# A gated MLP behind a state-space layer: the first tile of z2 starts among the last sums of v, and its sixteen tiles follow one order

## The chip, the cores and the metric

The kernel runs on one core of a Trainium2 chip. The time is what the device takes for one execution, in microseconds (us); for the kernel before it is 1783.14 us, the median of 3 runs (1782.89 to 1784.71).

Short names of the engines: PE is TensorE (PEld its weight loads), DVE is VectorE, ACT is ScalarE, POOL is GpSimd, SP is SyncE, which only issues transfers.

## The reference

One row of 2048 tokens with 576 channels goes through two layers. Cut to what matters here:

```
x = x + ga * SSM(layernorm(x) * (1 + ca) + sa)      # a convolution over the tokens
h = layernorm(x) * (1 + cb) + sb
z = gelu(h @ w_in)                                  # 2048 x 4608
z1, z2 = z[:, :2304], layernorm(z[:, 2304:])
g = w_sp @ z2 + b_sp[:, None]                       # mixes the 2048 tokens
x = x + gb * ((z1 * g) @ w_out)
```

The change concerns the end of the first layer and the making of z2: for every token, 2304 values of gelu(h @ w_in), and then a layernorm over them.

## The kernel before, in words

**Stages.** The first layer (function `ssm`) is computed by three small Fourier-like steps. Its last step are the sums of v: `y_unit(c, r)` multiplies the stored tensor v with a table on PE (16 small products, or 8 for the narrow fifth chunk `c4`), adds the old x on DVE, and POOL stores the new x1 in DRAM. `c` is one of five chunks of channels, `r` one of four groups of four tiles of 128 tokens. What a `y_unit` needs is loaded by SP: v by `y_vload`, the old x by `y_xload`. For the chunks `c3` and `c4` of the first group the sum goes straight into `x1f`, the buffer `xz` with the first four tiles' rows of x1 (4 x 576 values in each partition).

Next comes `phase_a`. It makes z2 in 16 tiles of 128 tokens, and while it does so prepares other weights on the side. `phase_b` then makes z1 (`z1_unit`), mixes the tokens (`g_products`) and multiplies with w_out.

**One tile b of z2.** The steps and the engines that they run on:

- `ln2_stats(b)`, `roots`, `ln2_rows(b)`: the layernorm of x1, on DVE. The result is the tile `n2` (`n` in the profile).
- `turn(b)`: five transposes on PE into the PSUM tile `pt`. `turn_hi(b)` copies them as float16 (tile `nt`) on ACT, and `turn_lo(b)` puts the rest that float16 leaves out beside it, on DVE.
- `z2_mm(b, h)`, h from 0 to 4: 14 products of 512 columns (256 for h = 4) on PE into a PSUM tile `pz`, of which there are six.
- `z2_gelu(b, h)`: gelu on ACT from `pz` into the SBUF tile `z2` of that token tile (2304 values in each partition, `z` in the profile). The first of them, h = 0, takes a fresh `z2` tile.
- `z2_stats(b, 0..5)`: statistics of z2 on DVE, the last two pieces after `z2_gelu(b, 4)`.
- `roots(b)`: 15 or so tiny operations on DVE that make the two factors of the layernorm. `z2_diff(b)`, for even b alone, subtracts one half of the tile from the other on DVE.
- `z2_norm(b)`: the layernorm itself on ACT, in place. `z2_store(b)`: two transfers of 576 KB that POOL issues, into `z2_d` in DRAM.

Tile b's `roots`, `z2_diff`, `z2_norm` and `z2_store` are written in the pass of the loop for tile b + 1. The pool `zp` of the `z2` tiles has two buffers. So `z2_gelu(b, 0)` cannot begin before the stores of tile b - 2 have landed.

**Side work.** In lists by tile (`side`, `do`), odd tiles take up a block of the left half of w_in: `side_sum` squares it on ACT ahead of `z2_gelu(b, 0)`; `win_scale` sums over partitions with a tiny product on PE ahead of `z2_mm(b, 1)` and makes a scale on DVE; `side_hi` and `side_lo` split the block on ACT and DVE. From tile 3 on ACT also squares pieces of other weights, two for each tile.

**What sets the order.** In the last part of `ssm` and in all of `phase_a` every instruction is pinned: each engine executes in the order in which the program writes it (`Pin`, whose line 132 stands for all of them in the profile). An engine that waits holds up all that is written behind it.

**The weights of z2.** w_in's right half is taken in five blocks of 512 columns: `start_load(q)`, `start_sum(q)` (ACT), `win_scale(5 + q)` (PE, DVE), `start_hi(q)` (ACT), `start_lo(q)` (DVE) make the float16 pair `wz`. Blocks 0 to 2 are done in `ssm`; 3 and 4 are finished beside tile 0 in `phase_a`.

Of the kernel before, what the change touches and what calls it, by code (L numbers as in the profile page):

```python
# [802 lines left out]
class Mlp:  # L803
# [450 lines left out]
    def phase_a(self):  # L1254
        self.prods, self.z1s, self.n2, self.bsp, self.gbs, self.wfs = {}, {}, {}, {}, {}, {}
        ap = self.ap = self.pool(self.c2, "ap", 2)
        cpa = ExitStack()
        self.pa = self.pool(cpa, "pa", 6, space=PSUM)
        self.ps1 = lambda: self.pa.tile([128, 512], F32, name="pz")
        self.zp = self.pool(self.c2, "zp", 2)  # L1260
# [58 lines left out]
        self.z2_mm(0, 0)
        self.start_sum(4)  # L1320
        self.z2_gelu(0, 0)
        self.z2_mm(0, 1)
        self.win_scale(9)
        self.start_hi(4)
        self.z2_gelu(0, 1)
        self.ln2_rows(1)
        self.z2_mm(0, 2)
# [401 lines left out]
```

## Time and profile before

| | before |
|---|---|
| median of 3 runs | 1783.14 us |
| the profiled execution, its time | 1782.85 us |
| the profiled execution, its span | 1781.1 us |
| PE busy | 1693.0 us, 95% of the span |
| DVE busy | 1127.6 us, 63% |
| ACT busy | 784.4 us, 44% |
| transfers, mean | 203 GB/s |

The profile is one execution, and what follows in the text is worked out within it; 1.75 us of its time lie outside the span. A row of the timeline has the start, the duration, the engine, the line (132 for all pinned work), the operation with out<-in, the shape, the count of merged instructions, and in brackets the engine's idle time before it and what ended it. Rows of one group that overlap are merged, so a row's duration over its count is the time from start to start. The durations are us, and those of page section 5 have a mean in ns. A table by windows gives each engine's busy us in a stretch, the granted clock of PE (1.00 is full) and the share of time in which the transfer engines were busy. In the lists of transfers "us to landing" counts from the end of the issue.

The stretch of interest lies between 415 us, where the last sums of v begin, and 698 us, where `g_products` begins. PE starts on z2 at 439.46 us and on z1 at 679.70 us.

### The profile page before, as it was taken

Reading aid. Unit: us, or ns where it says so; the run is one execution under the profiler, and the core shown is the slowest. Engines: PE = TensorE matmul, PEld = TensorE weight load, DVE = VectorE, ACT = ScalarE, POOL = GpSimd, SP = SyncE. Lnnn points to the kernel's source line nnn. Section 1 sums busy time; section 2 is a strip of 40 time slices with the busy share of each in tenths; the row PEclk is TensorE's granted clock in tenths of the full one; section 3 lists DMA queues with packets and bytes.
Section 4 is the critical chain, followed back from the end, with each engine's and each line's share of the span. In section 5 each row is a group of like instructions: output and inputs, shape, how many; then the busy total and the mean of one; then the engine's idle time right before and its main releaser. Section 6 shows DMA issues by size and latency. Waiting matters only on the chain.

```text
span 1781.1 us, 34047 instructions
## 1 busy us (share of the span) xinstructions
PE 1693.0 (95%) x14202; PEld 1195.6 (67%) x14202; DVE 1127.6 (63%) x2242; ACT 784.4 (44%) x1023; POOL 223.7 (13%) x350
## 2 busy tenths in 40 slices
PE   5688999997999999999999999999999999999999
PEld 1344555565455456877787777887778787787787
DVE  7988999868888997998783544483222274222322
ACT  5668999854576665554341322241211132011110
POOL 1221232342122110000000000000000000000000
PEclk8788999998999999999999999999999999999999
DMA  8457545799588888786554666563655572545520
GB/s 277 139 207 235 145 129 161 192 248 301 163 278 264 277 235 259 284 283 245 207 206 166 238 234 222 202 255 101 216 203 187 176 271 70 182 174 175 201 84 27
DMA packets 145866, 361.57 MB, mean 203 GB/s; under 512 B 23296, under 2 KB 59008, under 8 KB 143792
## 3 DMA queue, kind: packets, MB, share of 16 engines
q1 hardware_dynamic: 103104, 167.30, 29.8%
q0 software_dynamic: 33120, 153.95, 25.8%
q10 hardware_dynamic: 9488, 38.16, 5.4%
q8 instruction: 111, 1.82, 0.4%
q14 instruction: 43, 0.35, 0.1%
HBM read 256.86 MB, written 93.05 MB: 196 GB/s over the span
## 4 chain that ended last, share of the span: by engine, by line
PE 53%; issue 10%; DVE 9%; DMA 7%; ACT 2%; POOL 1%; SPq 0%; POOLq 0%; ACTq 0%; DVEq 0%
PE ps L1451 9%; PE ps L1453 9%; PE ps L1452 9%; PE ps L1416 9%; PE pz L132 4%; PE ps L1505 3%; PE ps L1506 3%; PE ps L1503 3%; DMA zset<-set_d 2%; DVE zset L1134 2%; DMA z_d<-z 1%; DVE bsz L132 1%; DVE gt L1466 1%; ACT z L132 1%; DMA gbs<-in_w_out 1%
## 5 line engine op out<-in xcount | busy, mean ns | idle before, releaser
L1451 PE MATMUL ps<-wsp,zset 128*128 128x256 f16 x2016 | 550.2, 273 | 2.9 <-DVE gt L1466 2.8
L1453 PE MATMUL ps<-wsp,zset 128*128 128x256 f16 x2016 | 550.1, 273 | 1.4 <-DVE zset L1134 1.3
L1452 PE MATMUL ps<-wsp,zset 128*128 128x256 f16 x2016 | 550.1, 273 | 0.0
L132 PE MATMUL pz<-wz,nt 128*128 128x512 f16 (+1 forms) x1120 | 224.2, 360 | 8.1 <-ACT nt L132 6.7
L1466 DVE SCALAR_TENSOR_TENSOR gt<-ps,sc,bsp 128x512 f32<-128x512 f32 x33 | 24.7, 749 | 317.2 <-PE ps L1453 317.2
L1416 PE MATMUL ps<-n2q,wf 128*128 128x512 f16 x1008 | 223.1, 379 | 0.0
L1451 PEld LDWEIGHTS <-zset 128*128 128x128 f16 x2016 | 197.7, 98 | 29.8 <-DVE gt L1466 3.0
L1452 PEld LDWEIGHTS <-zset 128*128 128x128 f16 x2016 | 197.5, 98 | 26.2
L1453 PEld LDWEIGHTS <-zset 128*128 128x128 f16 x2016 | 197.5, 98 | 25.0 <-DVE zset L1134 2.0
L132 PEld LDWEIGHTS <-nt 128*128 128x128 f16 x1120 | 109.5, 99 | 114.1 <-ACT nt L132 8.4
L1416 PEld LDWEIGHTS <-wf 128*128 128x128 f16 x1008 | 98.6, 98 | 111.8
L1428 POOL DMA_DIRECT2D zset<-set_d x96 | 50.8, 529 | 969.3 <-PE ps L1453 742.5
L1421 ACT ACTIVATE z<-ps,sc 128x512 f32<-128x512 f32 x56 | 37.8, 681 | 280.5 <-PE ps L1416 278.0
L1505 PE MATMUL ps<-wout,z 128*128 128x288 f16 x448 | 127.6, 286 | 0.0
L1506 PE MATMUL ps<-wout,z 128*128 128x288 f16 x448 | 127.6, 286 | 0.0
L1503 PE MATMUL ps<-wout,z 128*128 128x288 f16 x448 | 126.0, 286 | 1.0 <-ACT ot L1513 1.0
L1466 DVE SCALAR_TENSOR_TENSOR gt<-ps,sc,gt 128x512 f32<-128x512 f32 (+1 forms) x165 | 111.8, 694 | 5.4
L1134 DVE TENSOR_TENSOR zset<-raw,zset 128x1024 f16<-128x1024 f32 x48 | 58.5, 1220 | 75.2 <-ACT zset L1133 75.2
L1133 ACT ACTIVATE zset<-raw 128x1024 f16<-128x1024 f32 x48 | 50.3, 1050 | 99.6 <-PE ps L1453 69.7
L132 ACT ACTIVATE z<-pz,sc 128x512 f32<-128x512 f32 (+1 forms) x80 | 49.4, 647 | 54.1 <-DMA z_d<-z 43.6
L1521 DVE TENSOR_TENSOR ot<-ot,ps 128x288 f32<-128x288 f32 x31 | 14.0, 452 | 78.7 <-ACT ot L1513 78.7
L369 PE MATMUL ps<-ln_x,r1t 128*128 128x288 f32 x128 | 42.7, 490 | 18.9 <-issue 12.4
(360 smaller groups left out, 2830.6 us busy)
## 6 DMA issues: line engine op xcount, KB each, us to landing
zset<-set_d POOLq DMA_DIRECT2D x96, 896.0 KB, 4.8
set_d<-zset ACTq DMA_DIRECT2D x36, 896.0 KB, 5.8
raw<-z_d SPq DMA_DIRECT2D x48, 512.0 KB, 4.6
wf<-win_d SPq DMA_DIRECT2D x72, 320.0 KB, 3.5
raw<-in_w_spT SPq DMA_DIRECT2D x43, 512.0 KB, 6.3
z_d<-z POOLq DMA_DIRECT2D x32, 576.0 KB, 7.6
u_d<-st1o POOLq DMA_DIRECT2D x16, 576.0 KB, 4.5
u<-u_d SPq DMA_DIRECT2D x36, 256.0 KB, 4.7
```

The lines of the kernel that those rows point to most:

```text
L132: return self.tc.keep_in_program_order(f(*a, **k))
L1133: nc.scalar.activation(o[:, k, 0], t, AF.Copy)
L1134: nc.vector.tensor_tensor(o[:, k, 1], t, o[:, k, 0], op=ALU.subtract)
L1416: nc.tensor.matmul(pm.rearrange("p (t c) -> p t c", t=4), w[:, kw], self.n2[q][:, :, kn], start=i == 0, stop=i == len(Z1) - 1)
L1428: self.nc.gpsimd.dma_start(o, self.set_d[n // 4, n % 4])
L1451: T.matmul(pm, z[:, a, 0, c], w[:, b, 0], start=i + half == 0, stop=False, skip_group_check=True)
L1452: T.matmul(pm, z[:, a, 0, c], w[:, b, 1], start=False, stop=False, skip_group_check=True)
L1453: T.matmul(pm, z[:, a, 1, c], w[:, b, 0], start=False, stop=i == 7, skip_group_check=True)
L1466: V.scalar_tensor_tensor(dst, pm, inv, to, op0=ALU.mult, op1=ALU.add)
L1503: T.matmul(pl, p[:, 1, ts], w[:, 0, hs], start=st, stop=sp)
L1505: T.matmul(pa, p[:, 0, ts], w[:, 0, hs], start=st, stop=False)
L1506: T.matmul(pa, p[:, 0, ts], w[:, 1, hs], start=False, stop=sp)
```

## The change: what it does

1. `z2_mm(0, 0)` to `z2_mm(0, 2)` of the first tile move from `phase_a` into `ssm`. They stand among the last seven `y_unit`s: after `z2_mm(0, 0)` come three of them, after `z2_mm(0, 1)` two, after `z2_mm(0, 2)` two. `y_unit(c4, 0)`, the last part of the first tiles' rows, is taken ahead of `win_scale(8)`; `start_lo(2)` moves behind the first products. SP loads v for `c4` earlier and the old x of four `y_unit`s later.
2. PSUM changes hands at that place: the pool `psp` of `ssm` is closed, and the pool `pa` of `phase_a` opened, before `win_scale(8)`. The pools `zp` and `np` are opened earlier too, where the pool `wpre` is closed.
3. All tiles from 1 to 15 follow the order that only tile 1 had: `z2_mm(b, 1)`, `turn(b + 1)`, `z2_gelu(b, 1)`, `turn_hi(b + 1)` and `turn_lo(b + 1)` are written ahead of `roots(b - 1)`, `z2_diff`, `z2_norm(b - 1)` and `z2_store(b - 1)`.
4. The z2 tiles 2 and 5 use the buffer `x1f` instead of one of the two of `zp`. So tiles 3 to 7 wait for the stores of the tile three before them. From tile 8 on `x1f` holds blocks of w_sp, and the rotation is by two as before.
5. The three `nt` buffers are now two of `ap` and one of `np`.

The core of the diff:

```
+        first.close()
+        mlp.open_z2()
...
         y_unit(c2, 2)
         mlp.start_sum(3)
-        mlp.start_lo(2)
+        y_unit(c4, 0)
...
+        mlp.pair_stats(1)
+        mlp.ln2_rows(0)
+        banks.close()
+        ps1 = mlp.open_banks()
         mlp.win_scale(8)
+        mlp.turn(0)
+        mlp.turn_hi(0)
         mlp.start_hi(3)
+        mlp.turn_lo(0)
+        mlp.z2_mm(0, 0)
+        mlp.start_lo(2)
+        mlp.z2_gelu(0, 0)
+        for c, r in ((c2, 3), (c3, 1), (c4, 1)):
+            y_unit(c, r)
...
+        mlp.start_sum(4)
+        mlp.z2_mm(0, 1)
+        mlp.z2_gelu(0, 1)
+        mlp.start_lo(3)
+        y_unit(c3, 2)
+        y_unit(c4, 2)
+        mlp.win_scale(9)
+        mlp.start_hi(4)
+        mlp.z2_mm(0, 2)
+        mlp.z2_gelu(0, 2)
+        mlp.ln2_rows(1)
+        y_unit(c3, 3)
+        y_unit(c4, 3)
...
         if h == 0:
-            self.zs[b] = self.zp.tile([128, FH], F32, name="z2")
+            self.zs[b] = self.x1f.rearrange("p b d -> p (b d)") if b in (2, 5) else self.zp.tile([128, FH], F32, name="z2")
...
             self.z2_stats(b - 1, 5)
-            if b == 1:
-                do(b, PE)
-                self.z2_mm(b, 1)
+            do(b, PE)
+            self.z2_mm(b, 1)
+            if b + 1 < 16:
                 self.turn(b + 1)
-                self.z2_gelu(b, 1)
+            self.z2_gelu(b, 1)
+            if b + 1 < 16:
                 self.turn_hi(b + 1)
                 self.turn_lo(b + 1)
             self.roots(b - 1, b + 2 if b + 2 < 16 else None)
...
-            if b > 1:
-                do(b, PE)
-                self.z2_mm(b, 1)
-                if b + 1 < 16:
-                    self.turn(b + 1)
-                self.z2_gelu(b, 1)
             self.z2_store(b - 1)
             do(b, V0)
             self.z2_stats(b, 0, 1)
-            if 2 < b + 1 < 16:
-                self.turn_hi(b + 1)
-                self.turn_lo(b + 1)
             self.z2_mm(b, 2)
```

How instructions stand now, at three places. First PE at the start of z2. Before, the last of all sums (`ue` is v of chunk c4, `u` that of c3) stands right ahead of the transposes of tile 0 (`pt`):

```order
L132 MATMUL pk<-u_4585,st_1879 64x128
L132 MATMUL pk<-ue,st_1879 64x64 x8
L132 MATMUL pt<-ident,n_4616 128x128 x5
L132 LDWEIGHTS nt
L132 MATMUL pz<-wz,nt 128x512
```

Now it is the sum of c4 for the first group, and the tiny product of `win_scale(8)` follows it:

```order
L132 MATMUL pk<-u_4470,st_1879 64x128
L132 MATMUL pk<-u_4471,st_1879 64x128
L132 MATMUL pk<-ue,st_1879 64x64 x8
L132 MATMUL pz<-acc,ones 128x1
L132 MATMUL pt<-ident,n_4599 128x128 x5
L132 LDWEIGHTS n_4626
L132 MATMUL pz<-wz,n_4626 128x512
```

Seven sums that stood ahead of the transposes stand behind them.

Second ACT in tile 8. Before: two squares of side weights, `z2_gelu(8, 0)`, then `z2_norm(7)` (in place on the 2304 values of tile 7), `z2_gelu(8, 1)`, the two copies of `turn_hi(9)`, and the other gelus:

```order
L132 ACTIVATE wsst,acc<-wsst 128x864 x2
L132 ACTIVATE z_6053<-pz,sc 128x512
L132 ACTIVATE z_5867<-z_5867,nm_6075,r_6074 128x2304
L132 ACTIVATE z_6053<-pz,sc 128x512
L132 ACTIVATE nt<-pt 128x512
L132 ACTIVATE nt<-pt 128x128
L132 ACTIVATE z_6053<-pz,sc 128x512 x2
```

Now:

```order
L132 ACTIVATE wsst,acc<-wsst 128x864 x2
L132 ACTIVATE z_6054<-pz,sc 128x512 x2
L132 ACTIVATE n_6080<-pt 128x512
L132 ACTIVATE n_6080<-pt 128x128
L132 ACTIVATE z_5868<-z_5868,nm_6104,r_6103 128x2304
L132 ACTIVATE z_6054<-pz,sc 128x512 x2
```

The norm of tile 7 went from behind the first gelu to behind the second and behind `turn_hi(9)`.

Third DVE in tile 9. Before, the last statistics of tile 8 (`bsz`) are followed at once by `roots(8)` (`BN_AGGR` and what follows):

```order
L132 BN_STATS bsz<-z_6053 128x6 x2
L132 BN_AGGR mvx<-bsz 128x2
L132 TENSOR_SCALAR vh_6208<-mvx 128x2
L132 TENSOR_SCALAR rq_6209<-vh_6208 128x2
L132 TENSOR_SCALAR rx<-rq_6209 128x2
```

Now the end of the scale of `win_scale` and the two operations of `turn_lo(10)` (`nt<-pt`) stand right ahead of it:

```order
L132 TENSOR_TENSOR sc<-sc 128x1
L132 TENSOR_TENSOR nt<-pt,nt 128x512
L132 TENSOR_TENSOR nt<-pt,nt 64x128
L132 BN_AGGR mvx<-bsz 128x2
L132 TENSOR_SCALAR vh_6250<-mvx 128x2
```

`roots(b - 1)` moved behind `turn_lo(b + 1)` on DVE.

More of the change, by code (lines that the diff above doesn't have):

```diff
@@ L153, in ssm @@
         kp = ctx.enter_context(tc.tile_pool(name="kp", reuse_waits="tile", bufs=2, side="right"))
-        psp = ctx.enter_context(tc.tile_pool(name="psp", bufs=2, space=PSUM, reuse_waits="tile"))
+        banks = ctx.enter_context(ExitStack())
+        psp = banks.enter_context(tc.tile_pool(name="psp", bufs=2, space=PSUM, reuse_waits="tile"))
         early = ctx.enter_context(ExitStack())
@@ L619, in ssm @@
                 sb = ctx.enter_context(tc.tile_pool(name="sb", reuse_waits="tile", bufs=2, side="right"))
-                wpre = ctx.enter_context(tc.tile_pool(name="wpre", reuse_waits="tile", bufs=2, side="right"))
+                first = ctx.enter_context(ExitStack())
+                wpre = first.enter_context(tc.tile_pool(name="wpre", reuse_waits="tile", bufs=2, side="right"))
             if 9 <= tick < 13:
@@ L730, in ssm @@
         v_unit(c4, 3)
+        first.close()
+        mlp.open_z2()
         mlp.sum_two(2)
         y_vload(c2, 2)
-        for c, r in ((c2, 2), (c2, 3), (c3, 1), (c3, 2), (c3, 3), (c4, 1), (c4, 2), (c4, 3)):
+        y_xload(c2, 2)
+        y_vload(c4, 0)
+        for r in range(1, 4):
+            y_xload(c4, r)
+        for c, r in ((c2, 3), (c3, 1)):
             y_xload(c, r)
-        y_vload(c4, 0)
-        y_vload(c2, 3)
-        y_vload(c3, 1)
+            y_vload(c, r)
         y_vload(c4, 1)
+        mlp.start_load(4)
+        y_xload(c3, 2)
+        y_xload(c3, 3)
         mlp.start_rows()
         y_unit(c3, 0)
+        mlp.pair_stats(0)
         mlp.win_scale(7)
@@ L901, in start, with open_z2, open_banks @@
         self.stg = self.pool(self.c2, "stg", 2)
+    def open_z2(self):
+        self.zp = self.pool(self.c2, "zp", 2)
+        self.np = self.pool(self.c2, "np", 1)
+        self.ap = self.wzp
+    def open_banks(self):
+        self.cpa = ExitStack()
+        self.pa = self.pool(self.cpa, "pa", 6, space=PSUM)
+        self.ps1 = lambda: self.pa.tile([128, 512], F32, name="pz")
+        return self.ps1
     def start_x1(self):
@@ L1205, in turn_hi @@
         A, pm = self.nc.scalar, self.tps[b]
-        nt = self.nts[b] = self.ap.tile([128, 9, 128], F16, name="nt", bufs=3)
+        nt = self.nts[b] = self.ap.tile([128, 9, 128], F16, name="nt") if b % 3 else self.np.tile([128, 9, 128], F16, name="n0")
         A.activation(nt[:, 0:4], pm[:, 0].rearrange("p (k c) -> p k c", k=4), AF.Copy)
@@ L1256, in phase_a @@
         ap = self.ap = self.pool(self.c2, "ap", 2)
[L1257 to L1260, printed above, removed]
         self.wp = self.pool(self.ctx, "wp", 7, side="right")
@@ L1311, in phase_a @@
             side(12, LD, self.z1_load, 0, f)
-        self.turn(0)
-        self.turn_hi(0)
         self.x1_load(4)
-        self.turn_lo(0)
-        self.start_lo(3)
         do(0, LD)
[L1319 to L1327, printed above, removed]
         self.start_lo(4)
-        self.z2_gelu(0, 2)
         self.z2_mm(0, 3)
@@ L1387, in phase_a @@
             self.z2_gelu(b, 4)
-        cpa.close()
+        self.cpa.close()
         self.z2_stats(15, 5)
```

10 lines of the change are left out of this document (removed).

## The prediction, made before the changed kernel was run

> **What bounds the kernel now.** I read the page first: PE is busy for 95% of the span, so time is lost only where PE waits. Its groups name two such waits for z2 (line 132), and ACT's gelus wait mostly for the stores of z2.
>
> ```profile
> PE 1693.0 (95%) x14202; PEld 1195.6 (67%) x14202; DVE 1127.6 (63%) x2242; ACT 784.4 (44%) x1023; POOL 223.7 (13%) x350
> L132 PE MATMUL pz<-wz,nt 128*128 128x512 f16 (+1 forms) x1120 | 224.2, 360 | 8.1 <-ACT nt L132 6.7
> L132 ACT ACTIVATE z<-pz,sc 128x512 f32<-128x512 f32 (+1 forms) x80 | 49.4, 647 | 54.1 <-DMA z_d<-z 43.6
> ```
>
> Then the windows, for where PE is idle: 8.5 us of 20 ahead of z2, and almost nothing late in z2.
>
> ```profile
> 420.00:440.00 20.00, 11.46 (x139) 9.01 (x135) 15.69 (x48) 6.32 (x4) 5.56 (x8) 0.74 1.03 285
> 612.00:680.00 68.00, 65.53 (x349) 34.11 (x348) 61.37 (x185) 44.48 (x62) 12.37 (x14) 1.00 0.85 247
> ```
>
> Last PE's timeline. One tile without waits takes 14.2 us (462.08 to 476.24). The one large wait is 4.21 us, and the 14 products behind it take 4.88 us instead of 3.18.
>
> ```profile
> 440.91 6.22 PE L132 MATMUL pz<-wz,nt 128*128 128x512 f16 x28 [0.69 <-ACT nt L132]
> 447.11 6.20 PE L132 MATMUL pz<-wz,nt 128*128 128x512 f16 x28
> 453.15 0.71 PE L132 MATMUL pt<-ident,n 128*128 128x128 f32 x5
> 462.08 13.78 PE L132 MATMUL pz<-wz,nt 128*128 128x512 f16 x70
> 476.24 7.73 PE L132 MATMUL pz<-wz,nt 128*128 128x512 f16 x42
> 488.18 4.88 PE L132 MATMUL pz<-wz,nt 128*128 128x512 f16 x14 [4.21 <-ACT nt L132]
> 492.90 0.28 PE L132 MATMUL pz<-acc,ones 128*128 128x1 f32 x2
> 493.04 3.18 PE L132 MATMUL pz<-wz,nt 128*128 128x512 f16 x14
> ```
>
> A second loop runs beside PE's and is nearly as long. In tile 4: gelu(4,0) waits for store(2), then norm(3), then store(3); its landing releases gelu(5,0), and so on.
>
> ```profile
> 513.52 0.69 ACT L132 ACTIVATE z<-pz,sc 128x512 f32<-128x512 f32 x1 [5.80 <-DMA z_d<-z]
> 514.11 2.30 ACT L132 ACTIVATE z<-z,nm,r 128x2304 f32<-128x2304 f32 x1
> 516.31 0.68 ACT L132 ACTIVATE z<-pz,sc 128x512 f32<-128x512 f32 x1
> 516.70 2.02 POOL L132 DMA_DIRECT2D z_d<-z  x2 [8.13 <-ACT z L132]
> 569.68 0.69 ACT L132 ACTIVATE z<-pz,sc 128x512 f32<-128x512 f32 x1 [3.99 <-PE pt L132]
> 674.50 0.69 ACT L132 ACTIVATE z<-pz,sc 128x512 f32<-128x512 f32 x1 [4.37 <-DMA z_d<-z]
> ```
>
> From gelu to store it is 3.2 us there. From gelu(8,0) at 569.68 to gelu(15,0) at 674.50 the seven rounds take 104.8 us, 15.0 each: as long as PE needs with its small stops.
>
> **The change, part by part.** Part one, the front. PE's 8.5 idle us look free to fill, but tile 0 can't begin much earlier. Its rows need the sum of c4, whose v was stored at 416.26 and landed 6.71 us later.
>
> ```profile
> 416.26 6.71 DMA v_d<-ue
> 423.04 0.96 SPq L132 DMA_DIRECT2D ue<-v_d  x2
> 426.30 1.11 PE L132 MATMUL pk<-ue,st 128*64 128x64 f32 x14 [0.19 <-DMA ue<-v_d]
> 433.80 0.19 DVE L132 COPY n<-n 128x64 f32<-128x64 f32 x1
> 419.02 1.09 PE L132 MATMUL pk<-u,st 128*64 128x128 f32 x16
> x_d<-xb POOLq DMA_DIRECT2D x1, 256.0 KB, 3.4
> ```
>
> The rows are ready at 434.0; PE turns them only at 439.5, after seven sums. In the new order the sum's add on DVE no longer stands behind a scale (0.6 us gained), so rows at 433.4, then transposes (0.7), the copy (0.75) and their latencies: products at 435.2. Four old-x loads leave the queue ahead of that store; a store of the same size, issued alone at 421.7 (the last row, from the list of transfers), landed in 3.4 us. So perhaps 2.4 of the 6.71 us are saved: 432.8. Then come three groups of 3.05 us, a tiny product (0.2), seven sums (four of 1.0, three short ones of 0.85 to 0.9: 6.7) and a slow start after PE's long wait (4.88 − 3.18 = 1.7): group (0,3) begins at 450.5 to 452.9, where it now begins at 450.1 (453.15 − 3.05). The idle time is filled, but the slow start and the wait for c4 eat it. **I take +1 us**, bounds −1 and +3. The sums' adds lie on DVE between the splits of the weights; they delay nothing that PE asks for (start_lo(4) would end at 453.5, group (0,4) begins at 454).
>
> Part two, tiles 1 to 7. Tile 2 no longer waits for store(0), so the 4.21 us and the 1.7 behind them go. But norm(b−1) now stands behind turn_lo(b+1) and roots on DVE. Tile 1 already runs so:
>
> ```profile
> 462.32 0.76 ACT L132 ACTIVATE nt<-pt 128x512 f16<-128x512 f32 x2
> 466.42 1.02 DVE L132 TENSOR_TENSOR nt<-pt,nt 128x512 f16<-128x512 f32 x2
> 467.47 0.32 DVE L132 BATCH_NORM_AGGREGATE mvx<-bsz 128x2 f32<-128x36 f32 x1
> 470.94 1.36 DVE L132 TENSOR_TENSOR z<-z 128x1152 f32<-128x1152 f32 x1
> 472.40 1.35 ACT L132 ACTIVATE z<-z,nm,r 128x1152 f32<-128x1152 f32 x1 [9.32 <-DVE z L132]
> 475.18 2.03 POOL L132 DMA_DIRECT2D z_d<-z  x2 [6.67 <-ACT z L132]
> 479.79 1.05 ACT L132 ACTIVATE wsst<-wsst 128x1024 f32<-128x1024 f32 x1
> 489.68 2.37 ACT L132 ACTIVATE wso<-wst 128x2560 f16<-128x2560 f32 x1
> ```
>
> turn_lo takes 1.05, roots 3.5 (467.47 to 470.94), the difference 1.3, norm and issue 2.8. What is queued behind norm(b−1) on ACT: gelus 2 to 4, and then the square that the next odd tile's win_scale needs on PE ahead of its second group. Tile 2 laid out: ACT is through the side squares at 480.8; gelu(2,0), gelu(2,1), turn_hi(3) to 482.7; turn_lo(3) to 483.7; roots to 487.1; norm(1) to 489.4; three gelus to 491.2; the square to 493.6. PE, unstalled, has finished group (3,0) at 487.1 and asks then: it waits 5 to 6.5 us. So the wait only changes its place, and group (3,1) begins where it does now (493.04). For tile 5 the same gives the square at 20.2 us after the start of tile 4 and PE's question at 17.3: 3 us, and 3 again in tile 7. With +1 from the front, tile 7 begins at 456.3 + 6 × 14.2 + 5 + 3 = 549.5. In it store(6) is issued after 3.05 + 3 + 0.2 + 3.05 + 0.55 + 0.2 (products, wait, transposes) and 0.75 + 1.05 + 3.5 + 1.3 + 2.4 + 0.3: 19.3 us, at 568.8. With a landing of L = 9 us (below) gelu(8,0) begins at 577.8, now 569.68: **+8 us** with the front.
>
> Part three, tiles 8 to 15, the largest. They rotate by two buffers, so gelu(b,0) waits for store(b−2), and store(b−1) now stands behind gelu(b,0), gelu(b,1) (0.57 each), turn_hi (0.75), turn_lo (1.05), roots (3.5), norm (2.2) and the issue (0.3): 8.9 us, and 10.4 where the difference comes first. The new round is that plus L. PE's 14.2 lie beside it, and ACT's and DVE's other work of a tile too. Queued on ACT behind the wait for store(b−2) is turn_hi(b+1), for which PE's next tile waits, and behind norm(b−1) the gelus 2 to 4, which free the six PSUM tiles: so PE goes at this round's pace. How long L is, from the issue to the gelu, shows in these rows:
>
> ```profile
> 589.90 2.02 POOL L132 DMA_DIRECT2D z_d<-z  x2 [11.08 <-ACT z L132]
> 597.91 0.69 ACT L132 ACTIVATE z<-pz,sc 128x512 f32<-128x512 f32 x1 [1.46 <-DMA z_d<-z]
> 605.48 2.02 POOL L132 DMA_DIRECT2D z_d<-z  x2 [8.10 <-ACT z L132]
> 617.34 0.69 ACT L132 ACTIVATE z<-pz,sc 128x512 f32<-128x512 f32 x1 [4.26 <-DMA z_d<-z]
> 664.42 2.01 POOL L132 DMA_DIRECT2D z_d<-z  x2 [9.96 <-ACT z L132]
> ```
>
> 8.0, 11.9 and 10.1 us. The slower round thins the other traffic, so I take 9, towards the shortest. Rounds: 4 × 8.9 + 3 × 10.4 + 7 × 9 = 129.8, against 104.8: **+25 us**. Each us of L is 8 us of time (the first store and seven rounds).
>
> Part four, the handover. Tile 15 has no turn behind it, so what follows gelu(15,0) keeps its order. z2's first set is complete 19.4 us after gelu(15,0).
>
> ```profile
> 692.94 0.95 DVE L1134 TENSOR_TENSOR zset<-sum,zset 128x768 f16<-128x768 f32 x1
> 697.83 0.27 PE L1451 MATMUL ps<-wsp,zset 128*128 128x256 f16 x1
> ```
>
> Now PE is still busy with z1 then and starts at 697.83, 23.3 after it. In the changed kernel PE, early, is done with tile 15 and z1 by that time, and starts at 19.5: **−4 us**. Phase B itself is unchanged.
>
> Sum: 8 + 25 − 4 = +29, on the profiled execution's 1782.85 us (span 1781.1 and 1.75 around it; the median is 1783.14): **1812 us**.
>
> **The rivals.** First, on the other side: the stores land so fast that PE sets the pace. With 9.6 us on the engines on average it decides at L = 4.6. Then it is 8 − 4.4 + 7 × 14.2 − 104.8 − 3.8 = −5.6: 1777. Against it: the shortest L in the trace is 8.0. The Trainium skill, "DMA: Bandwidth & Descriptors", section "Anatomy of one DMA — SWDGE (gpsimd) path", fits 2.0 us plus bytes over 436 GB/s, which would be an estimate of 4.7 us for the 1.18 MB of a store, and so this rival's time. The trace does not agree: 8.0 us at best, amid other transfers.
>
> Second, the landing stays long, 11 to 12 us as at 605.48, since loads and stores still meet: 8 × 2 to 8 × 3 more, 1828 to 1836. For it: the transfer engines are 0.85 busy; against it: that comes from a faster round.
>
> Third, the change doesn't do what it says: `x1f` isn't free when tile 2 wants it, and the slow round holds from tile 2 on. Six more rounds of 18.6 instead of 15 to 16: about 1830. Against it: the rows' stores and reads end a round earlier.
>
> Fourth, no change: L = 6 with the stops of tiles 5 and 7 gone, 1812 − 24 − 6 = 1782. It needs both, and L = 6 lies below every row.
>
> **How the numbers follow.** Forecast 0.79; fast landing 0.06; long landing 0.08; `x1f` late 0.04; no change 0.03. The range reaches from L = 8 with the 6 us of stops in tiles 5 and 7 gone (1812 − 8 − 6 = 1798) to L = 10 with a late front (1812 + 8 + 2) and a little into the second rival: 1798 to 1826. What a measurement can tell from no change is about 0.2%, 3.6 us. Faster 0.06, the same 0.03, slower 0.91.
>
> **What would show it.** Right: PE's z2 products begin near 433 to 435, with sums between them, and z1 begins near 709 instead of 679.7. In tiles 9 to 15 gelu(b,0) follows its predecessor by 18 to 19.5 us and is released by a store of z2, and store(b−1) is issued 9 to 10.5 us after gelu(b,0), not 3 to 6. Before groups (3,1), (5,1) and (7,1) PE waits for ACT's square. Wrong: rounds of 14 to 15 us in tiles 9 to 15, which would refute part three; gelu(3,0) to gelu(7,0) released by stores, which would be the third rival; the first set of z2 late by something other than gelu(15,0).

## The result, and the profile after

The changed kernel takes **1844.39 us** (median of 6 runs, 1841.08 to 1849.17) against 1783.02 us (1782.49 to 1789.42) before: a ratio of **1.0339, 95% interval 1.0318 to 1.036**. The forecast was 1812 us, range 1798 to 1826. Slower was right; the loss is twice the size forecast.

The profiled execution of the changed kernel has a span of 1843.4 us. Here it is cut at four points that every variant has: the total behind the last sums of the last group of v (PE, `sums,ones`), gelu(8,0), gelu(15,0) and the end.

| stretch, us | before | forecast | after | after less forecast |
|---|---|---|---|---|
| start to the total of the sums | 418.7 | 418.7 | 416.1 | −2.6 |
| to gelu(8,0) | 151.0 | 159.1 | 170.5 | +11.4 |
| gelu(8,0) to gelu(15,0) | 104.8 | 129.8 | 140.1 | +10.3 |
| gelu(15,0) to the end | 1106.6 | 1102.8 | 1116.7 | +13.9 |
| span | 1781.1 | 1810.4 | 1843.4 | +33.0 |

(The forecast column is the prediction's own: gelu(8,0) at 577.8, rounds of 129.8, and 19.5 + 1083.3 behind gelu(15,0).)

The first stretch lies ahead of everything that was changed. In the sixteen profiles of this study it takes 416 to 425 us, so spans and single times carry some 9 us that are no one's doing. The other three stretches are what I compare. They scatter too: the kernel before and the kernels of runs 13 and 14 execute the same instructions up to gelu(15,0), and their profiles take 151.0, 152.7 and 155.6 us to gelu(8,0), and 104.8, 105.7 and 104.7 us from there to gelu(15,0). A difference of less than 5 us in the first of these two stretches is therefore not shown by a pair of profiles.

The page's row of PE and its groups of z2's products and gelus (tiles whose buffers have other names stand in groups of their own):

```profile
PE 1713.2 (93%) x14202; PEld 1197.8 (65%) x14202; DVE 1127.9 (61%) x2242; ACT 785.4 (43%) x1023; POOL 223.5 (12%) x350
L132 PE MATMUL pz<-wz,nt 128*128 128x512 f16 (+1 forms) x700 | 149.3, 374 | 10.3 <-ACT nt L132 10.3
L132 PE MATMUL pz<-wz,n 128*128 128x512 f16 (+1 forms) x420 | 93.9, 385 | 5.2 <-ACT n L132 5.2
L132 ACT ACTIVATE z<-pz,sc 128x512 f32<-128x512 f32 (+1 forms) x70 | 41.7, 634 | 55.7 <-DMA z_d<-z 33.3
```

The same products take 149.3 + 93.9 = 243.2 us; they took 224.2. PE did not only wait more, its products were slower: 374 and 385 ns against 360. The timeline shows where. **Tiles 3, 5 and 7**, PE, the total that `win_scale` asks for and the group behind it:

```profile
490.71 0.59 PE L132 MATMUL pz<-acc,ones 128*128 128x1 f32 x2 [6.17 <-ACT wso L132]
491.16 5.94 PE L132 MATMUL pz<-wz,n 128*128 128x512 f16 x14
...
526.66 0.38 PE L132 MATMUL pz<-acc,ones 128*128 128x1 f32 x2 [4.25 <-ACT wso L132]
526.90 4.87 PE L132 MATMUL pz<-wz,nt 128*128 128x512 f16 x14
...
560.47 0.38 PE L132 MATMUL pz<-acc,ones 128*128 128x1 f32 x2 [3.40 <-ACT wso L132]
...
560.94 4.87 PE L132 MATMUL pz<-wz,nt 128*128 128x512 f16 x14
```

The 14 products behind each wait take 4.9 to 5.9 us instead of 3.18. The windows say why (columns: the stretch, its length, busy PE, PEld, DVE, ACT, POOL with counts, then the granted clock, the transfers' share, GB/s):

```profile
482.00:485.00 3.00, 2.55 (x12) 0.98 (x10) 2.58 (x14) 0.48 (x1) 0.10 (x1) 1.00 0.25 98
491.20:494.20 3.00, 3.00 (x9) 1.07 (x10) 1.56 (x10) 2.24 (x5) 0.00 (x0) 0.50 1.04 326
494.20:497.00 2.80, 2.80 (x9) 1.07 (x8) 0.00 (x0) 0.00 (x0) 0.00 (x0) 0.54 0.79 261
526.90:529.90 3.00, 3.00 (x11) 1.20 (x11) 1.79 (x10) 2.48 (x5) 0.00 (x0) 0.60 1.03 307
```

Ahead of the wait the granted clock is 1.00; behind it 0.50, 0.54 and 0.60. The Trainium skill, "TensorE: Matmul & The Clock Gate", section "Part 1: The HAM clock gate", says that the clock goes to half after an idle window of about 3.4 us and comes back after as long a busy one. The trace agrees for these: the waits of 4.25 and 6.17 us are followed by 3 to 6 us at half clock or little more. It is not so for every wait: in tile 13 PE waits 3.79 us (at 669.50), and the 14 products behind it take 3.19 us.

**Tiles 8 to 15.** ACT and POOL in tile 9 and at the start of tile 10:

```profile
595.70 2.02 POOL L132 DMA_DIRECT2D z_d<-z  x2 [5.01 <-ACT z L132]
607.24 1.27 ACT L132 ACTIVATE z<-pz,sc 128x512 f32<-128x512 f32 x2 [4.25 <-DMA z_d<-z]
608.40 0.77 ACT L132 ACTIVATE nt<-pt 128x512 f16<-128x512 f32 x2
614.97 1.35 ACT L132 ACTIVATE z<-z,nm,r 128x1152 f32<-128x1152 f32 x1 [5.81 <-DVE z L132]
617.76 2.06 POOL L132 DMA_DIRECT2D z_d<-z  x2 [6.48 <-ACT z L132]
627.09 1.26 ACT L132 ACTIVATE z<-pz,sc 128x512 f32<-128x512 f32 x2 [3.40 <-DMA z_d<-z]
```

This is the predicted round: gelu(9,0), gelu(9,1), turn_hi(10), a wait for DVE's roots and difference, the norm, the store 10.5 us after gelu(9,0), its landing, gelu(10,0). All seven rounds are released by a store; 140.1 / 7 = 20.0 us each. L, from the issue to the gelu, is 11.5, 9.3, 11.1, 10.0, 9.2, 10.3 and 10.8 us: 10.3 on average.

**The handover** has two waits that I had not seen coming. PE, ACT, POOL and, in the last row, DVE of the changed kernel:

```profile
713.12 13.78 PE L132 MATMUL pz<-wz,n 128*128 128x512 f16 x70
733.59 14.97 PE L1426 MATMUL ps<-n2q,wf 128*128 128x512 f16 x56 [6.70 <-ACT z L132]
738.98 2.31 ACT L132 ACTIVATE z<-z,nm,r 128x2304 f32<-128x2304 f32 x1 [5.44 <-DVE nm L132]
741.58 2.01 POOL L132 DMA_DIRECT2D z_d<-z  x2 [8.93 <-ACT z L132]
751.01 1.84 ACT L1431 ACTIVATE z<-ps,sc 128x512 f32<-128x512 f32 x3 [9.72 <-DMA z_d<-z]
754.81 0.27 PE L1461 MATMUL ps<-wsp,zset 128*128 128x256 f16 x1
754.97 0.95 DVE L1170 TENSOR_TENSOR zset<-sum,zset 128x768 f16<-128x768 f32 x1
```

PE, done with tile 15, waits 6.70 us for that tile's last gelu before it can start on z1. z1's 84 products then take 21.4 us (18.3 in the kernel before), with a wait of no more than 0.2 us between them, and the mixing follows at once. On ACT, z1's first gelus (line 1431; the `z` of that row is a z1 tile) wait 9.72 us for z2's last store. They neither read nor write z2. The first set (`zset`) is made behind them, so it is complete only at 755.92, 29.2 us after gelu(15,0). In the kernel before the gelus follow the norm at once:

```profile
686.78 2.31 ACT L132 ACTIVATE z<-z,nm,r 128x2304 f32<-128x2304 f32 x1 [5.43 <-DVE nm L132]
688.99 1.82 ACT L1421 ACTIVATE z<-ps,sc 128x512 f32<-128x512 f32 x3
```

### The profile page after: what moved, and what is told of

It reads as the page before. It is cut to its first block, busy times and chain, and to the rows that moved or that the text cites. A ratio compares the mean times of both kernels' runs of the same rounds, so it can differ in the third digit from the quotient of the medians.

```text
span 1843.4 us, 34035 instructions
## 1 busy us (share of the span) xinstructions
PE 1713.2 (93%) x14202; PEld 1197.8 (65%) x14202; DVE 1127.9 (61%) x2242; ACT 785.4 (43%) x1023; POOL 223.5 (12%) x350
## 4 chain that ended last, share of the span: by engine, by line
PE 47%; DVE 5%; issue 5%; DMA 4%; ACT 1%; SPq 0%; POOL 0%; ACTq 0%; DVEq 0%; POOLq 0%
PE ps L1461 10%; PE ps L1463 10%; PE ps L1462 10%; PE ps L1426 9%; PE ps L1516 3%; PE ps L1513 3%; PE ps L1515 3%; DVE zset L1170 2%; DMA gbs<-in_w_out 1%; DMA z_d<-z 1%; DVE gt L1476 1%; DMA zset<-set_d 1%; DMA gbs<-mod_d 0%; ACT z L132 0%; DMA xz<-in_w_spT 0%
## 5 line engine op out<-in xcount | busy, mean ns | idle before, releaser
L1426 PEld LDWEIGHTS <-wf 128*128 128x128 f16 x1008 | 99.2, 98 | 121.1 <-issue 10.5
L132 PE MATMUL pz<-wz,nt 128*128 128x512 f16 (+1 forms) x700 | 149.3, 374 | 10.3 <-ACT nt L132 10.3
L132 PEld LDWEIGHTS <-nt 128*128 128x128 f16 x700 | 70.7, 102 | 82.4 <-issue 11.6
L132 PE MATMUL pz<-wz,n 128*128 128x512 f16 (+1 forms) x420 | 93.9, 385 | 5.2 <-ACT n L132 5.2
L132 PEld LDWEIGHTS <-n 128*128 128x128 f16 x420 | 43.3, 105 | 51.5 <-issue 11.8
L132 ACT ACTIVATE z<-pz,sc 128x512 f32<-128x512 f32 (+1 forms) x70 | 41.7, 634 | 55.7 <-DMA z_d<-z 33.3
```

The source lines that it names most:

```text
L132: return self.tc.keep_in_program_order(f(*a, **k))
L1426: nc.tensor.matmul(pm.rearrange("p (t c) -> p t c", t=4), w[:, kw], self.n2[q][:, :, kn], start=i == 0, stop=i == len(Z1) - 1)
```

## The experiments

All medians beside their own runs of the kernel before; ratios with 95% intervals; the last three columns are stretches of the profiled execution.

| run | time, us | ratio | to gelu(8,0) | to gelu(15,0) | to the end |
|---|---|---|---|---|---|
| before | 1783.02 | | 151.0 | 104.8 | 1106.6 |
| after | 1844.39 | 1.0339 (1.0318–1.036) | 170.5 | 140.1 | 1116.7 |
| 1 loop of before | 1787.3 | 1.0023 (1.0008–1.0039) | 147.4 | 105.3 | 1115.0 |
| 2 front alone | 1793.03 | 1.0044 (1.0028–1.006) | 152.6 | 105.3 | 1113.7 |
| 3 loop of before from tile 8 | 1806.7 | 1.0124 (1.0098–1.015) | 173.5 | 102.5 | 1112.8 |
| 4 totals later | 1837.37 | 1.0294 (1.0267–1.0322) | 161.1 | 137.8 | 1112.6 |
| 5 z1 moved | 1838.71 | 1.031 (1.0289–1.0332) | 171.2 | 140.1 | 1107.2 |
| 6 loop of before, z1 moved | **1780.63** | **0.9976 (0.9962–0.9991)** | 148.3 | 105.1 | 1101.6 |
| 7 loop alone | 1854.92 | 1.0383 (1.0357–1.0409) | 192.0 | 137.4 | 1105.6 |
| 8 fewer loads | 1843.22 | 1.0333 (1.0313–1.0353) | 174.1 | 133.3 | 1112.7 |
| 9 z1 and banks moved | 1839.04 | 1.0301 (1.0255–1.0347) | 174.1 | 143.6 | 1105.6 |
| 10 stores from ACT | 1855.52 | 1.0387 (1.0349–1.0425) | 181.9 | 135.9 | 1115.8 |
| 11 long rows | 1822.55 | 1.0202 (1.0158–1.0246) | 169.6 | 116.5 | 1112.2 |
| 12 as 6, stores from ACT | 1801.58 | 1.0082 (1.0053–1.011) | 155.2 | 105.5 | 1118.2 |
| 13 before, z2's pool first | 1793.39 | 1.0041 (1.0024–1.0057) | 152.7 | 105.7 | 1113.2 |
| 14 before, z1 moved | 1785.12 | 0.9997 (0.9978–1.0016) | 155.6 | 104.7 | 1101.9 |

### 1. The loop of before, in the changed kernel

```
-            do(b, PE)
-            self.z2_mm(b, 1)
+            if b == 1:
+                do(b, PE)
+                self.z2_mm(b, 1)
...
+            if b > 1:
+                do(b, PE)
+                self.z2_mm(b, 1)
...
             self.z2_store(b - 1)
```

> The changed kernel with the tile loop of the kernel before (group (b,1) and the turn behind the norm, for b over 1); the front and `x1f` for tiles 2 and 5 stay. Theory: the loop order is the cause of the whole loss, the front costs about nothing and `x1f` takes away the stop of tile 2. Then the time is that of before or a little below: 1776 to 1784 us; gelu(8,0) comes at 562 to 570 us, and gelu(8,0) to gelu(15,0) is 104 to 106 us. Rival: the front, or where the PSUM tiles now lie, is part of the loss (handover +4.8, the end of the program +5.3): 1788 to 1800 us.

Measured 1787.3 us: outside the theory's range and just under the rival's. The stretches split it. Up to gelu(8,0) the time is the theory's, 147.4 us against 151.0; the rounds are those of before, 105.3. The reason is not the theory's: gelu(2,0) no longer waits for a store, but PE's stop in tile 2 is still there, 3.60 us where it was 4.21, because turn_hi(3) stands behind norm(1), which waits for DVE:

```profile
487.65 4.88 PE L132 MATMUL pz<-wz,n 128*128 128x512 f16 x14 [3.60 <-ACT n L132]
```

And 8.4 us are lost behind gelu(15,0), with z1's gelus again behind the store:

```profile
683.25 2.31 ACT L132 ACTIVATE z<-z,nm,r 128x2304 f32<-128x2304 f32 x1 [5.43 <-DVE nm L132]
693.89 1.84 ACT L1441 ACTIVATE z<-ps,sc 128x512 f32<-128x512 f32 x3 [8.33 <-DMA z_d<-z]
```

PE stands still for the first set meanwhile, and the windows behind show the price of it:

```profile
697.47 0.39 PE L1471 MATMUL ps<-wsp,zset 128*128 128x256 f16 x1 [3.03 <-ACT zset L1169]
698.00:704.00 6.00, 5.21 (x28) 3.73 (x28) 6.00 (x11) 3.51 (x5) 0.00 (x0) 0.53 0.81 298
704.00:720.00 16.00, 16.00 (x149) 14.35 (x147) 15.13 (x25) 9.07 (x12) 0.00 (x0) 1.00 0.82 299
```

28 products in 6 us at a clock of 0.53, then 149 in 16 us at 1.00. So the loop order is not the whole loss; something in the kept part moves z1 behind the store. What has moved is SBUF: the change opens z2's pool `zp` ahead of phase A's pool `ap`, where it lay behind it, and the z1 tiles of phase B come to lie on its buffers. That was the theory for the runs that follow.

### 2. The front alone

As run 1, and

```
-            self.zs[b] = self.x1f.rearrange("p b d -> p (b d)") if b in (2, 5) else self.zp.tile([128, FH], F32, name="z2")
+            self.zs[b] = self.zp.tile([128, FH], F32, name="z2")
```

> As the run with the loop of before, and tiles 2 and 5 in the rotation of the two z2 buffers again, so that the front alone is left of the change. Theory: the front is worth +1 us (bounds -1 to +3), so 1782 to 1786 us, and the wait for store(0) in tile 2 (about 4 us on PE) is back. Rival, that the front itself costs: 1788 us and more.

Measured 1793.03 us: by the time alone the rival is right. By the stretches the front costs 152.6 − 151.0 = 1.6 us, within the bounds and within the scatter; 7.1 are lost behind gelu(15,0), the loss of run 1. Run 13, which has that loss and no front, takes as long (1.0041 against 1.0044), so no cost of the front itself is seen. The buffer `x1f` for tiles 2 and 5 (run 1 against this one, both on the same chip) is worth 5.7 us in the medians and 152.6 − 147.4 = 5.2 us up to gelu(8,0). It isn't the stop in tile 2 that it saves, which is 3.92 us here and 3.60 there, but shorter ones of 0.4 to 0.9 us, in tiles 5 to 12, that are gone there.

### 3. The loop of before from tile 8 on

```
-            do(b, PE)
-            self.z2_mm(b, 1)
+            if b < 8:
+                do(b, PE)
+                self.z2_mm(b, 1)
...
+            if not (b < 8):
+                do(b, PE)
+                self.z2_mm(b, 1)
```

> The changed kernel with the loop of before from tile 8 on; tiles 1 to 7 keep the new order. Theory: the store loop of tiles 8 to 15 is a loss of its own (+35 in the trace of after), and tiles 1 to 7 lose 17 by the stops at the totals: 1800 to 1806 us, gelu(8,0) at 583 to 588 us, rounds of 15 us behind it. Rival: the later rounds are long for another cause than the order (transfers that meet, the banks): still 20 us a round, 1835 us and more.

Measured 1806.7 us, 0.7 above the theory's range. Rounds of 102.5 / 7 = 14.6 us again: the order alone makes the 35 us of tiles 8 to 15. The loss of tiles 1 to 7 stays whole, 173.5 us (170.5 in the changed kernel).

### 4. The totals a group later

```
-            side(2 * q + 1, PE, self.win_scale, q)
+            side(2 * q + 1, V0, self.win_scale, q)
```

> The changed kernel with the totals of win_scale (tiles 1, 3, 5, 7, 9) ahead of group (b,2) instead of group (b,1), so that PE asks for the side square a group of 3.05 us and the turn later. Theory: tiles 3, 5 and 7 lose 5 to 6 us each there (the wait and the slow products behind it), and half or more of that goes: gelu(8,0) at 570 to 578 us instead of 586.7, total 1828 to 1836 us; the rounds of tiles 9 to 15 stay at 20 us. Rival: PE is held there by the round through the store anyway and only waits elsewhere: 1841 us and more, gelu(8,0) at 584 us or later.

Measured 1837.37 us, 1.4 above the range, and gelu(8,0), counted from the sums, 9.4 us earlier (expected: 8.7 to 16.7). PE in tiles 3, 5 and 7:

```profile
492.49 0.38 PE L132 MATMUL pz<-acc,ones 128*128 128x1 f32 x2 [1.14 <-ACT wso L132]
...
524.32 0.58 PE L132 MATMUL pz<-acc,ones 128*128 128x1 f32 x2 [3.10 <-ACT wso L132]
...
556.07 0.38 PE L132 MATMUL pz<-sums,ones 128*128 128x1 f32 x2 [3.63 <-DVE sums L132]
```

The waits are 1.14, 3.10 and 3.63 us in place of 6.17, 4.25 and 3.40. The third is another one: the sum of w_sp's squares on DVE, which hid behind the total in the changed kernel. Tiles 8 to 15 hardly change (137.8 us): there the store's round sets the pace.

### 5. z1 out of z2's buffers

In `phase_b`, so that only places in SBUF change:

```
-        self.wout = bp.tile([128, 18, 2, D], F16, name="wout")
+        bp.tile([128, 2, 512], F32, name="z1", bufs=7)
+        bp.tile([128, 2, 512], F32, name="gt", bufs=1)
+        bp.tile([128, 2, 512], F32, name="z1b", bufs=2)
+        bp.tile([128, 128], F32, name="pad")
...
         self.wsp_build(0, 7)
+        self.wout = bp.tile([128, 18, 2, D], F16, name="wout")
```

> The changed kernel; only where the tiles of phase B lie in SBUF is other: the z1 tiles (with gt and z1b) swap places with wout, so that z1 no longer lies over the buffers of z2. Theory, formed after the run with the loop of before: the change opens the pool of z2 ahead of the pool of phase A, so z2's buffers lie lower, and the first z1 tiles come to lie on them; z1's first gelu then waits for the landing of z2's last store (9.7 us in the trace of after, none in before), PE waits for the first set, and its first products are slow. So z1's gelu comes right behind norm(15), the first product of phase B 20 to 25 us after gelu(15,0) instead of 28.1, the rest of phase B takes 1083 to 1085 us instead of 1088.6: 1830 to 1837 us. Rival: z1 is held by its PSUM bank (PE waits 6.7 us for gelu(15,4)) or by the store itself: 1841 us and more.

Measured 1838.71 us, between the two. z1's gelu now follows the norm, and from gelu(15,0) to the end it takes 1107.2 us instead of 1116.7. But the first product comes at 757.12, 28.8 us after gelu(15,0), no earlier than in the changed kernel, because PE waits for something else:

```profile
735.23 17.61 PE L1426 MATMUL ps<-n2q,wf 128*128 128x512 f16 x70 [7.14 <-ACT z L132]
740.63 2.31 ACT L132 ACTIVATE z<-z,nm,r 128x2304 f32<-128x2304 f32 x1 [5.44 <-DVE nm L132]
742.84 0.67 ACT L1431 ACTIVATE z<-ps,sc 128x512 f32<-128x512 f32 x1
```

Two waits lay side by side; one is gone, the other decides when z1 starts. The gain lies behind the first product, where the rest of phase B takes 1078.4 us instead of 1088.6, more than the theory had.

### 6. Run 1 with z1 moved

> The loop of before, the front and `x1f` of the change, and z1 out of z2's buffers as in the run beside it. Theory: what made the first run 1.0023 is only the place of z1 (some 8 us at the handover and behind it), and tile 2 without its stop is worth 3.5 us: 1776 to 1781 us, ratio 0.996 to 0.999. Rival: the front costs: 1785 us and more.

Measured 1780.63 us, ratio 0.9976 with an interval that ends below 1: it **beats both kernels**. From gelu(15,0) to the end 1101.6 us instead of run 1's 1115.0, and run 1's gain up to gelu(8,0) is kept, 148.3 against 151.0. PE's stop in tile 2 is here too (4.05 us), so it is not that stop which the theory's 3.5 us come from.

### 7. The loop alone, in the kernel before

> The kernel before with the new tile loop alone: no front, no `x1f`, pools as before. Theory: with two buffers from tile 2 on, the round through the store (9.6 us on the engines and 10.4 of landing) holds from tile 2 on: gelu(2,0) to gelu(15,0) takes 13 rounds of 19 to 20 us, 250 to 260 us instead of 191; the handover is at its better place. 1838 to 1858 us, slower than after. Rival: in tiles 2 to 7 the stops at the totals set the pace either way, and `x1f` is worth nothing: 1822 to 1834 us.

Measured 1854.92 us, in the theory's range: slower than the changed kernel. The new order without `x1f` takes 192.0 us to gelu(8,0), 41 more than before; with it 170.5. The end, 1105.6, is that of before: no overlap here.

### 8. Fewer loads beside the stores

```
+        if i >= 4:
+            return
         return self.nc.sync.dma_start(t, self.I["w_out"]...
...
+        if q != 1 or pool is None:
             self.wsp_read(t, q, i)
```

> The changed kernel without the loads of w_out from the fifth piece on and of the second block of w_spT in phase A (8 of 442 KB and 6 of 524 KB, in tiles 8 to 14); their sums of squares are taken from a tile of ones, so the scale of w_out and of that block is not the real one. All else is issued as before. Theory: the landing L is long (10.4 us) because stores meet these loads; without them L is 7 to 8.5 us, each us 8 us of time: rounds of 17 to 18.5 us, 1817 to 1829 us. Rival: L is the store's own time (two issues, 1.18 MB, the write's acknowledgement): rounds of 19.5 us and more, 1838 us and more.

The time fell by 1 us only, 1843.22. The rounds fell by 6.8 us, to 133.3 / 7 = 19.0 each, with L at 9.35 us on average (8.7 to 11.0, the shortest an upper bound, since PE released that gelu). So neither theory gets its round: 6.7 MB of loads make one us of L's ten. The start of this profile is 8.8 us later than that of after, ahead of the edit; whether that hides the gain in the median too I can't tell. The slope of the prediction holds: 0.97 us of L less, times seven rounds, is 6.8 us.

### 9. z1 and the PSUM banks

As run 5, and

```
         self.ps1 = lambda: self.pa.tile([128, 512], F32, name="pz")
+        self.pa.tile([128, 2, 512], F32, name="pt", bufs=1)
```

> As the changed kernel with z1 out of z2's buffers; also the two PSUM banks of the transposes (pt) are taken ahead of the six of the products (pz), as in the kernel before. There z1's first products now wait 7.1 us for the gelu of the last group of tile 15, since z1's first bank is that group's. Theory: the handover needs both places right; with both, z1's products follow tile 15's at once and the first product of phase B comes 20 to 23.5 us after gelu(15,0) instead of 28.8: 5 to 8 us less than with z1 moved alone, 1829 to 1834 us. Rival: z2's last store holds the first set by itself: 28 us again, 1837 us and more.

The mechanism came out as the theory has it: z1 starts without a wait, and the first product of phase B comes 18.0 us after gelu(15,0).

```profile
738.89 6.21 PE L1427 MATMUL ps<-n2q,wf 128*128 128x512 f16 x28
...
759.13 0.28 PE L1462 MATMUL ps<-wsp,zset 128*128 128x256 f16 x1 [0.52 <-ACT zset L1170]
...
760.58 0.28 PE L1464 MATMUL ps<-wsp,zset 128*128 128x256 f16 x1 [1.06 <-DVE zset L1171]
```

The time did not: 1839.04 us, as run 5 and in the rival's range. From gelu(15,0) to the end it is 1105.6 against 1107.2 there; the 10.8 us that the first product gained are mostly given back behind it, where the rest of phase B takes 1087.6 us instead of 1078.4. The traces show where: from the first product on PE waits 9.1 us here and 1.9 in run 5; 7.2 of the 9.1 are for sets and for `gt` that DVE has yet to finish. The longest of the waits,

```profile
927.23 0.28 PE L1462 MATMUL ps<-wsp,zset 128*128 128x256 f16 x1 [2.95 <-DVE gt L1477]
```

is followed by two stretches of 3.4 us with a granted clock of 0.62 and 0.88, some 1.7 us more by my estimate; with the 7.2 us of waits that run 5 doesn't have, that is nearly the whole difference of 9.2. Started earlier, PE catches up with DVE.

### 10. The stores issued from ACT

```
-            self.nc.gpsimd.dma_start(self.z2_d[...
+            self.nc.scalar.dma_start(self.z2_d[...
```

> The changed kernel with z2's two stores of a tile issued from ACT's queue instead of POOL's. Leaving other loads out shortened the landing L only from 10.3 to 9.5 us. Theory: some 2 us of L are the two issues of 1.0 us each on POOL; from ACT an issue takes 0.35 us, so L is 8 to 9 us, rounds of 18.5 to 19.2 us, 1832 to 1839 us. Rival: L is the transfer of 1.18 MB in rows of 512 bytes and its acknowledgement, whoever issues it: rounds of 19.7 us and more, 1841 us and more.

Measured 1855.52 us, a ratio of 1.0387 where the changed kernel has 1.0339 (the intervals overlap). An issue on ACT takes more than 0.35 us: of a tile's two the first takes 0.4, the second 0.6 to 2.5, together 1.0 to 2.9 us, 1.4 in the median. POOL's two take 2.0. PE at the total of tile 3, and one of the long pairs:

```profile
498.46 0.59 PE L132 MATMUL pz<-acc,ones 128*128 128x1 f32 x2 [8.85 <-ACT wso L132]
...
610.45 2.46 ACTq L132 DMA_DIRECT2D z_d<-z  x2
612.96 1.63 ACT L132 ACTIVATE z<-pz,sc 128x512 f32<-128x512 f32 x3 [2.54 <-issue]
```

The issues stand on the engine whose squares PE waits for: ahead of the totals of tiles 3, 5, 7 and 9 PE now waits 8.85, 7.80, 6.22 and 9.22 us instead of 6.17, 4.25, 3.40 and 6.57, and gelu(8,0) comes 11.4 us later after the sums. The landings, 8.3 us in the median (10.9 from `x1f`), are not shorter than POOL's 8.1 (9.7). L is 10.0 us on average (7.5 to 13.3) and a round 135.9 / 7 = 19.4, between the theory's and the rival's. So the change of issuer shortens L by 0.3 us, not by the 1.3 to 2.3 of the theory.

### 11. Long rows in DRAM

```
-            self.nc.gpsimd.dma_start(self.z2_d[:, b // 4, :, 2 * (b % 2) + h, b % 4 // 2].rearrange("f p c -> p f c"), z[:, h])
+            self.nc.gpsimd.dma_start(flat[:, h], z[:, h].rearrange("p f c -> p (f c)"))
```

> The changed kernel with z2 stored in DRAM in rows of 4608 bytes (tile after tile) instead of 512 bytes scattered by channel; the same bytes and as many issues. Phase B then reads other values than it should, by the same loads as before. Theory: the short rows make the store slow (200 to 330 GB/s when it is nearly alone); long ones land in 7 to 8.5 us instead of 10.3: rounds of 17 to 18.5 us, 1818 to 1831 us. Rival: the rows make no difference and L is latency and issue: 1841 us and more.

Measured 1822.55 us, in the theory's range. The list of transfers (issues, KB each, median us to landing), of the changed kernel and of this one. The traces show that these us count from the start of each issue, not from its end as said ahead of the prediction:

```profile
z_d<-z POOLq DMA_DIRECT2D x28, 576.0 KB, 8.1
```

```profile
z_d<-z POOLq DMA_DIRECT2D x28, 576.0 KB, 5.7
```

The same bytes, 2.4 us sooner. Some 0.5 us of that is the issue on POOL, which halves: 1.07 us for two instead of 2.02. From gelu(13,0) on the round is no longer released by a store; store(11) has landed 0.7 us ahead of it, and ACT doesn't wait:

```profile
595.79 1.07 POOL L132 DMA_DIRECT2D z_d<-z  x2 [5.01 <-ACT z L132]
605.42 1.26 ACT L132 ACTIVATE z<-pz,sc 128x512 f32<-128x512 f32 x2 [3.02 <-DMA z_d<-z]
...
671.43 1.26 ACT L132 ACTIVATE z<-pz,sc 128x512 f32<-128x512 f32 x2
```

116.5 us for seven rounds, 16.6 each, below the theory's 17: two thirds of the loss of tiles 8 to 15 are gone. The edit changes the length of the rows and with it their number and their places in DRAM; which of these it is, the run doesn't separate. The Trainium skill, "DMA: Bandwidth & Descriptors", section "Specifications", holds 512 bytes for enough to run at full rate. The measurement differs for these stores: between the rows of 512 and those of 4608 bytes lie 2.4 us of 8.1.

### 12. Run 6 with the stores from ACT

> The loop of before, the front and `x1f` of the change, z1 out of z2's buffers (1780.6 us in its run), and z2's stores issued from ACT. Theory: this loop is close to PE's pace (15.0 us a round against 14.2 of products and turn), so a landing shorter by 1 to 2 us gains at most 0.8 us a round, 5 us in all: 1774 to 1780 us. Rival: the issue on ACT (0.7 us a tile) stands ahead of turn_hi and gelus and costs as much: 1780 to 1786 us.

Measured 1801.58 us, longer than theory and rival had it. To gelu(8,0) it takes 155.2 us instead of run 6's 148.3, and the end 1118.2 instead of 1101.6, where PE waits for a weight of z1:

```profile
712.86 6.04 PE L1436 MATMUL ps<-n2q,wf 128*128 128x512 f16 x14 [6.45 <-DMA wf<-win_d]
```

How the place of the stores' issue delays that load was not traced.

### 13. and 14. The kernel before with other places in SBUF

Run 13 moves one line of the kernel before; run 14 is the edit of run 5 in the kernel before.

```
+        self.zp = self.pool(self.c2, "zp", 2)
         ap = self.ap = self.pool(self.c2, "ap", 2)
...
-        self.zp = self.pool(self.c2, "zp", 2)
```

> The kernel before; z2's pool is opened ahead of phase A's pool instead of behind it, one line moved, so that z2's buffers lie lower in SBUF and the first z1 tiles of phase B come to lie on them. Not one instruction is other or in another place. Theory: z1's first gelu waits for the landing of z2's last store, and from gelu(15,0) to the end it takes 1112 to 1116 us instead of 1106.6: 1789 to 1793 us, ratio 1.003 to 1.006. Rival: it takes the front or the new loop too to lose there: 1781 to 1786 us.

> The kernel before; z1, gt and z1b swap places with wout in SBUF, as in the version that beat both kernels. Theory: z1 didn't lie on z2's buffers before, so this is worth nothing: 1782 to 1785 us, and the 0.24% of that version come from tile 2 without its stop. Rival: the other place is itself the gain: 1777 to 1781 us.

Run 13 takes 1793.39 us, ratio 1.0041 (1.0024 to 1.0057), and 1113.2 us from gelu(15,0) to the end. Its z1 waits as in the changed kernel:

```profile
690.46 2.31 ACT L132 ACTIVATE z<-z,nm,r 128x2304 f32<-128x2304 f32 x1 [5.43 <-DVE nm L132]
701.34 1.85 ACT L1421 ACTIVATE z<-ps,sc 128x512 f32<-128x512 f32 x3 [8.57 <-DMA z_d<-z]
704.92 0.28 PE L1451 MATMUL ps<-wsp,zset 128*128 128x256 f16 x1 [3.24 <-ACT zset L1133]
```

So the overlap alone, without front, loop or `x1f`, lengthens the last stretch. In all nine profiles with z1 over a buffer of z2 it takes 1112 to 1117 us, and with z1 elsewhere 1102 to 1107, run 12 with its late weight left aside. Run 14 is no change, 0.9997 (0.9978 to 1.0016). So the gain of run 6 is more likely that of `x1f` (5.7 us between runs 1 and 2) than the place's. It isn't settled: the two intervals overlap, and run 14's last stretch is as short as run 6's, 1101.9 and 1101.6 us against 1106.6. In its profile the way to gelu(8,0), which the edit doesn't touch, is longer by as much.

## Why the prediction was right or wrong

**The front, +1: right.** z2's products begin at 430.19, 14.1 us behind the total of the sums instead of 22.2 (440.91), with the sums between them, and group (1,0) begins 36.7 us behind it, where it was 36.5. Run 2 puts the front's cost at 1.6 us, which is within the scatter. The store of c4's v landed sooner, as argued: its reader is issued 1.8 us behind that total, where it was 4.3.

**Tiles 2 to 7, "the wait only changes its place": the place was right, the sum was mis-sized.** PE waits for ACT's square ahead of groups (3,1), (5,1) and (7,1). I priced them at 5, 3 and 3 us; they are 6.17, 4.25 and 3.40. Worse, I left out the slow products behind them, 2.76, 1.69 and 1.69 us, though I had quoted such a row (4.88 against 3.18) and counted it in the front. Tile 7 so begins 7 us later than forecast: 6.17 + 2.76 + 4.25 + 1.69 = 14.9 instead of 8. In tile 7 itself store(6) is issued 21.9 us after the start, not 19.3, and lands in 10.9, not 9. That is the 11.4 us of this stretch. Run 4 shows that the waits are the cause: less of them, and gelu(8,0) comes 9.4 us sooner. PE's stop of 4.21 us in tile 2 went as forecast (tile 3 begins 65.2 us behind the total of the sums, where it was 69.5), but not because store(0) is no longer waited for: run 1 has `x1f` and keeps 3.60 us of it, run 7 has the new order without `x1f` and keeps 1.42. It is the order that removes it.

**Tiles 8 to 15, +25: the mechanism right, L mis-sized.** The round is the one laid out; its part on the engines is (140.1 − 72.2) / 7 = 9.7 us, forecast 9.5. Run 3 shows that the order makes it, run 7 that it does so by itself. The failed term is "I take 9, towards the shortest" for L: 10.3 measured, 1.3 more, and over seven rounds that is 9.2 of the 10.3 us. My reason, that a slower round thins the other traffic, was right about the traffic and wrong about L: between 569 and 675 us the transfer engines are busy for 0.66 of the time, where it was 0.83, and yet L is no shorter than in the kernel before, whose seven stores there average 9.8. Run 8 took 6.7 MB of loads away and won one us. What makes L long lies more in the store itself and its rows of 512 bytes (run 11). The rival of the long landing named 11 to 12 us and, as the cause, transfers that meet, which run 8 shows to be worth about one us; the fast-landing rival is refuted, since even behind tile 15, beside 0.76 MB of weights alone, the store took from 741.58 to 751.01.

**The handover, −4: wrong in sign.** The failed steps are "what follows gelu(15,0) keeps its order" and "PE, early, is done with tile 15 and z1 by that time". The order is kept, the places are not, in two memories. In PSUM, z1's first bank is now the one of tile 15's last group: PE is early, as forecast, but waits 6.70 us for that group's gelu, goes on slowly and is done with z1 only at 754.8. In SBUF, z1's tiles lie on a buffer that z2's last store still reads: ACT waits 9.72 us with z1's gelus, and the first set behind them is complete 29.2 us after gelu(15,0) instead of 19.4. Each of the two holds the first product by itself: it comes 28.1 us after gelu(15,0) instead of the 19.5 forecast, 28.8 with z1 moved in SBUF alone (run 5), 18.0 with both places right (run 9), and 26.7, where it was 23.3, with the SBUF place alone wrong (run 13). These 8.6 us are the larger part of the 13.9. The other 5.3 lie behind the first product and go with the SBUF place: the rest of phase B takes 1088.6 us, and 1078.4 in run 5. That the first set comes late by something other than gelu(15,0) was named beforehand as a sign of being wrong. The moved lines `open_z2` and `open_banks` stand in the diff; I costed their waits at nothing and did not ask what would lie on those addresses later. Nor would the −4 have come with the places right: in run 9 the whole stretch takes 1105.6 instead of before's 1106.6, 1 us, because PE then waits for DVE in phase B.

**`x1f` late for tile 2** (third rival): refuted, gelu(3,0) to gelu(7,0) aren't released by stores, and in run 7, without the buffer, the way to gelu(8,0) is 21.5 us longer than in the changed kernel. **No change:** refuted, it needed L = 6.

## What to carry to other kernels

A diff that opens a pool earlier moves addresses: ask for every tile allocated later which buffer it now lies on and which transfer still reads it; one moved line cost 0.4% with no instruction changed. Ask the same of PSUM banks. Where PE waits 3 us and more, add the slow group behind it, here 1.7 to 2.9 us, to most such waits (eight of the nine in the changed kernel between 485 and 735 us). Where a store closes a loop, price its landing by the mean of the profile's rows, and look at its row length as well as at its neighbours.
